# Linear attention into a three-matrix FFN on one core: w3 @ w_out moved from tile 0 to the front, and the start replanned

## The chip, the cores and the metric

The kernel runs on one core of a Trainium2 chip. The metric is the device time of one execution in microseconds (us). Engines are called PE (matmul), PEld (its weight load), DVE (VectorE), ACT (ScalarE), POOL (GpSimd) and SP (SyncE).

## The reference

Inputs are float32. q, k, v are [8 batches, 8 heads, 576 positions, 64]; w1, w2 are [512, 1024], w3 is [1024, 1024], w_out is [1024, 512].

```python
def phi(x, c, s):
    r = np.maximum(x, 0.0)
    return np.concatenate([r * c, r * s], axis=-1)      # 128 features
q_p, k_p = phi(q, cos_w, sin_w), phi(k, cos_w, sin_w)   # cos, sin of pi/2 * position / 576
kv  = np.einsum('bhsf,bhsd->bhfd', k_p, v)
z   = np.sum(k_p, axis=2)
num = np.einsum('bhsf,bhfd->bhsd', q_p, kv)
den = np.einsum('bhsf,bhf->bhs', q_p, z)[..., None] + 1e-06
x   = (num / den).transpose(0, 2, 1, 3).reshape(4608, 512)
out = (((x @ w1) * (x @ w2)) @ w3) @ w_out              # [4608, 512]
```

## The kernel before

**The algebra.** w3 @ w_out is computed once ("w34", 1024 x 512), so that a token costs three products: x @ w1, x @ w2 and their elementwise product @ w34. All matmuls are bfloat16 with float32 sums in PSUM.

**Attention.** A batch's 576 positions are five chunks, four of 128 and one of 64. Per chunk, `features` makes cos * relu on DVE and sin * relu on ACT (`kp`, `qp`), `prep_v` copies v beside a column of ones (`va`), and `kv_chunk` adds eight heads' 65-column products into PSUM. After the fifth chunk the sums are cast to `kvs`, one half on ACT, one on DVE. `q_tr` transposes a chunk of `qp` on PE (or a DMA does, `transpose_q`), the copy out of PSUM is `qpT`; `num` multiplies it with `kvs` and normalises on DVE (`den`, its reciprocal, `xblk`); `x_tr` transposes `xblk` on PE, copied to `xT` by ACT or DVE, or by a DMA on SP's queue for batches 2 and later. With `in_two`, `num` uses two FFN banks and normalises each by itself.

**FFN.** Nine tiles of 512 tokens. `ffn_groups(t)` is a generator: it issues a group of matmuls and yields. For each of eight column blocks `jc` there is x @ w1 (cast by ACT to `asb`) and x @ w2 (multiplied with `asb` by DVE into `abT`), and then four output blocks against `w34b`, each in two groups of four matmuls. Tile 0 and tile 1 take their first products in halves of 256 tokens (`on_half`), tile 0 some of them in quarters of 128, so that they can start on the first chunks of x. FFN results use four PSUM banks in turn (`ffn_tile`).

**w34 in the kernel before.** Inside tile 0, after its products, `w34_mm(jp, part)` runs eight blocks of eight 512-column matmuls. `w3_tr(jp)` transposes w3's row block jp by eight PE transposes into `pst`, and DVE copies them to `w3T`. ACT casts each sum to `w34b`.

**Order.** The schedule is manual: every engine works in the order in which the program issues its instructions. `slots[g]` is a list of calls made after FFN group g; `at(s, ...)` and `plan(b, ...)` put the attention steps of later batches into slots. Tile 0 has 40 groups and every later tile 24. `plan` takes slot lists: kf and qf for the features of k and q, vc for `prep_v`, kv for `kv_chunk`, nu for `num`, xt for `x_tr`.

**Loads.** POOL issues the loads, which cast float32 to bfloat16 on the way; only batch 0's k (`kf`, float32) comes on SP's queue. The order is k, v, q of batch 0, then the first halves of w1 and w2, then (after the first chunk's `xblk`) the rest of w1 and w2, w3 in row blocks with w_out between, batch 1. `plan_loads` places later batches' loads in slots, held back until ACT reaches that point (`hold_back`).

**The start.** 27 matmuls on zeros (`idle_mms`, into the tile `unread`) run on PE while the first loads come; then kv of batch 0 (`kv_first`), q's transposes, `num` and `x_tr` of chunk 0, and tile 0.

Of the kernel before, what the change touches and what calls it, by code (L numbers as in the profile page):

```python
# [10 lines left out]
FP32 = mybir.dt.float32  # L11
# [5 lines left out]
P = 128  # L17
H, S, D = 8, 576, 64
F = 2 * D
NCH = 5  # L20
# [48 lines left out]
def kernel(  # L69
# [30 lines left out]
    first = [ctx.enter_context(ExitStack()) for _ in range(2)]  # L100
    ps_idle = first[1].enter_context(tc.tile_pool(name="ps_idle", bufs=1, space=bass.MemoryType.PSUM))
    ps_first = first[0].enter_context(tc.tile_pool(name="ps_first", bufs=1, space=bass.MemoryType.PSUM))
# [42 lines left out]
    def load_wout(half):  # L145
        nc.gpsimd.dma_start(out=woutb[:, ts(half, 4), :],
                            in_=moe_w_out[ts(half, 512), :].rearrange("(c p) m -> p c m", p=P))

    k0 = raw[0, "k"] = wst.tile([P, H, NCH, D], FP32, name="kf")
    q0 = raw[0, "q"] = ld.tile([P, H, NCH, D], BF16, name="qs", bufs=2)  # L150
    v0 = raw[0, "v"] = ld.tile([P, H, NCH, D], BF16, name="vs")
    load_first(nc.sync, k0, k)
    load_first4(nc.sync, k0, k)
    load_first(nc.gpsimd, v0, v)
# [19 lines left out]
    unread = ps_idle.tile([P, 512], FP32, name="unread")  # L174
    kva = ps_idle.tile([P, 512], FP32, name="kva")

    def idle_mms(n):

        for _ in range(n):
            nc.tensor.matmul(unread[:, :], lhsT=zeros[:, 0:128], rhs=zeros[:], start=True, stop=True)  # L180

    idle_mms(27)
    cosv, sinv = _trig_tables(nc, const)
    identb = const.tile([P, P], BF16, name="identb")
    load_first4(nc.gpsimd, v0, v)
    load_first(nc.gpsimd, q0, q, 0, 2)
    make_identity(nc, identb[:])
    load_first(nc.gpsimd, q0, q, 2, 2)
    def load_w12(c0, n):
        nc.gpsimd.dma_start(out=w1b[:, :, ds(c0, n)], in_=w1v[:, :, ds(c0, n)])  # L190
        nc.gpsimd.dma_start(out=w2b[:, :, ds(c0, n)], in_=w2v[:, :, ds(c0, n)])
# [4 lines left out]
    nc.gpsimd.dma_start(out=w1b[:, :, ds(512, 256)], in_=w1v[:, :, ds(512, 256)])  # L196

    def other_loads(behind):

        seen = sm.tile([P, 1], BF16, name="seen", bufs=1)  # L200
        nc.gpsimd.tensor_copy(out=seen[:], in_=behind)
        nc.gpsimd.dma_start(out=w2b[:, :, ds(512, 256)], in_=w2v[:, :, ds(512, 256)])
        load_w12(768, 256)
        for jp in range(2):
            load_w3(jp, 1)
            load_wout(jp)
        for jp in range(2, 4):
            load_w3(jp, 1)
        load_w3(4, 2)
        load(1, "k")  # L210
        load_w3(6, 2)

# [11 lines left out]
    w34_acc = {}  # L224

# [11 lines left out]
    def order_of(b):  # L237

        return [0, 1, 2, 3, 4] if b % 2 == 0 else [4, 0, 1, 2, 3]
# [48 lines left out]
    def prep_v(b, c):  # L288
        R = ROWS[c]
        eng = nc.vector if b < 2 else nc.gpsimd  # L290
        eng.tensor_copy(out=feat_of(b)[2][:R, c, :, 0:D], in_=raw[b, "v"][:R, :, c, :])  # L291
# [15 lines left out]

    def kv_first():

        kp, qp, va = feat[0]  # L310
        kvs = sm.tile([P, H, D + 1], BF16, name="kvs", bufs=2)
        kvb = ps_att.tile([P, 2, 512], FP32, name="pnum")
        halves = (kva[:, :], kvb[:, 0, :])
        for c in range(NCH):
            for h in range(H):
                nc.tensor.matmul(halves[h // 4][:, ds((h % 4) * 65, 65)], lhsT=kp[:, c, h, :],
                                 rhs=va[:, c, h, 0:D + 1], start=(c == 0 and h % 4 == 0),
                                 stop=(c == NCH - 1 and h % 4 == 3))
        att_of(0)["kvs"] = kvs
        yield  # L320
        for half in range(2):
            nc.scalar.copy(out=kvs[:, 4 * half:4 * half + 4, :], in_=halves[half][:, 0:260])
        yield
# [23 lines left out]
    def num(b, c, chain=True, in_two=False):  # L347
# [4 lines left out]
        if b == 0 and c == 0:  # L352
            nt = ps_first.tile([P, 2, 512], FP32, name="pfirst")
        else:
            pool = more_att[0] if more_att and order_of(b).index(c) % 2 == 0 else ps_att
            nt = None if in_two else pool.tile([P, 2, 512], FP32, name="pnum")
# [86 lines left out]
    ffn_tiles = [0]  # L443

    def ffn_tile():
        pool = ps_ffn[ffn_tiles[0] // 2 % 2]
        ffn_tiles[0] += 1
        return pool.tile([P, 512], FP32, name="ffnps")

    def ffn_groups(t):  # L450
# [14 lines left out]

        def on_half(half):

            if half == 1 and t == 0:
                banks = [(ffn_tile(), ffn_tile()) for _ in range(2)]
                for quarter in range(2):  # L470
                    for pair, (a, b) in enumerate(banks):
                        for i in range(2):
                            for ps, w in ((a, w1b), (b, w2b)):
                                products(ps[:, ds(256 * i + 128 * quarter, 128)], w, 2 * pair + i,
                                         ds(256 + 128 * quarter, 128))
                        if quarter == 1:
                            multiply(a, b, pair, half)
                        if quarter == 0 or pair == 1:
                            yield
                return  # L480
            for pair in range(2):
                a, b = ffn_tile(), ffn_tile()
                if pair == 0 and t == 0:
                    for quarter in range(2):
                        for i in range(2):
                            for ps, w in ((a, w1b), (b, w2b)):
                                products(ps[:, ds(256 * i + 128 * quarter, 128)], w, i,
                                         ds(256 * half + 128 * quarter, 128))
                            if half == 0 and quarter == 0 and i == 0:
                                yield  # L490
                        if quarter == 0:
                            yield
                else:
                    for ps, w in ((a, w1b), (b, w2b)):
                        for i in range(2):
                            products(ps[:, ts(i, 256)], w, 2 * pair + i, ts(half, 256))
                        if w is w1b and (t == 1 or half == 0):
                            yield
                multiply(a, b, pair, half)
                yield  # L500

        if t < 2:
            yield from on_half(0)
            yield from on_half(1)
        for jc in range(4 if t < 2 else 0, 8):
# [9 lines left out]
        if t == 0:  # L515
            for jp in range(8):
                for part in range(2):
                    w34_mm(jp, part)
                    yield
            early.close()  # L520
            holds.append(ctx.enter_context(tc.tile_pool(name="hold", bufs=HELD,
                                                        reuse_waits="tile")))
# [28 lines left out]
    slots = [[] for _ in range(40 + 24 * (NT - 1))]  # L551
# [31 lines left out]
    for c in range(NCH):  # L583
        prep_k(0, c)
    for c in range(NCH):
        prep_v(0, c)
    kv_steps = kv_first()
    next(kv_steps)
    q0f = feat[0][1]
    features(0, q0f, q0, 0, scalar_heads=4)  # L590
    next(kv_steps)
    prep_q(0, 1)
    idle_mms(2)
    q_tr_halves(0, 0)
    prep_q(0, 2)
    idle_mms(1)
    num(0, 0)
    q_tr(0, 1, evac=False)[1]()
    other_loads(att[0]["x"][0][:, 0, 0, 0:1])
    features(0, q0f, q0, 3, sin=False)  # L600
    features(0, q0f, q0, 3, cos=False)
    idle_mms(2)
    x_tr(0, 0, by_vector=True)
    num(0, 1)
    q_tr(0, 2, evac=False)[1]()
    ps_ffn = []
    for stack in first:
        stack.close()
    for i in range(2):
        ps_ffn.append(ctx.enter_context(tc.tile_pool(name=f"ps_ffn{len(ps_ffn)}", bufs=2,  # L610
                                                     space=bass.MemoryType.PSUM)))


    at(1, lambda: x_tr(0, 1, by_vector=True), lambda: q_tr(0, 3, evac=False)[1](), lambda: num(0, 2))
    at(3, lambda: x_tr(0, 2), lambda: num(0, 3))
    at(5, lambda: x_tr(0, 3))
    at(6, lambda: features(0, q0f, q0, 4))
    at(23, lambda: transpose_q(0, 4))
    at(7, lambda: load(1, "qv"), lambda: load(2, "q"))
    at(29, lambda: num(0, 4))  # L620
    at(11, lambda: feature_buffers(1))
    at(29, lambda: x_tr(0, 4))

    for jp, s in enumerate((13, 16, 18, 20, 22, 24, 26, 28)):
        at(s, lambda jp=jp: w3_tr(jp))

    plan(1, kf=(24, 25, 26, 27, 28), vc=(31, 31, 32, 32, 32), kv=(33, 33, 33, 34, 34),
         qf=(29, 30, 30, 31, 31), nu=(35, 36, 38, 39, 42), xt=(37, 38, 40, 42, 42))
    for c, s in zip(order_of(1), (31, 32, 34)):
        at(s, lambda c=c: q_tr(1, c))  # L630
    at(43, no_more_by_pe)
# [59 lines left out]
```

## Time and profile before

| what | value |
|---|---|
| median of 3 runs | 249.66 us (249.4 to 249.91) |
| profiled execution, its own time | 249.83 us |
| its span, first to last instruction | 248.1 us |
| granted TensorE clock, mean | 0.999 |
| DVE, ACT, POOL busy | 137.5, 130.5, 93.3 us |
| x @ w1 and x @ w2, PE (L456) | 2 x 75.5 us |
| output products, PE (L526) | 65.1 us |
| w3 @ w_out, PE (L231) and w3's transposes (L219) | 15.8 and 4.9 us |
| matmuls on zeros, PE (L180) | 32, 9.4 us |
| HBM read, written | 38.80 MB, 9.44 MB |

A group row tells line, engine, operation, tiles, shape and count, then busy time, mean ns of one, idle time before it and what ended that. A row of the order in time tells start and length in us first; rows of the chain too. A row of the waits tells who waited for whom, us in total, how often, and the longest. A matmul's length holds the pipeline's tail, so the pace of queued matmuls is read from start to start: a 512-column one 0.216 us, a 128-column transpose 0.056, a 65-column one 0.032.

### The profile page before, as it was taken

The page shows a single profiled execution, that of the slowest core. Times are in us where ns is not written, and L with a number is a line of the kernel's source. Part 1 is how long each engine was busy: PE and PEld are TensorE (multiplying, and loading weights), DVE is VectorE, ACT ScalarE, POOL GpSimd, SP SyncE. Part 2 cuts the span into 40 slices and gives each one's busy share as a digit, 9 for nine tenths or more (in the row PEclk, how much of TensorE's full clock was granted, in tenths as well). Part 3 has the DMA queues.
Part 4 walks back from the last instruction along what each step waited for, and adds up shares of the span by engine and source line. Part 5 has one row for each costly group of instructions (what it writes and reads, how often), then busy time and mean ns, then how long its engine had stood idle before and what let it go on. Part 6 is the DMA issues. An engine that isn't in the chain of part 4 may idle for free.

```text
span 248.1 us, 5041 instructions
## 1 busy us (share of the span) xinstructions
PE 240.9 (97%) x1872; PEld 130.1 (52%) x1872; DVE 137.5 (55%) x336; ACT 130.5 (53%) x266; POOL 93.3 (38%) x196
## 2 busy tenths in 40 slices
PE   8899999999999999999999999999999999999993
PEld 3479445566964445545554545455445544444442
DVE  7875653668967544656665475657455644403320
ACT  2675323867933963476447654754575234334322
POOL 7655342124412351217122612352222006968600
PEclk9999999999999999999999999999999999999999
DMA  6999999999989979999999999999996427999925
GB/s 199 178 194 199 201 194 204 198 194 175 144 151 148 167 117 151 130 142 103 170 160 173 117 160 169 160 119 144 157 138 112 91 42 242 264 290 276 295 55 127
DMA packets 84744, 41.22 MB, mean 166 GB/s; under 512 B 52336, under 2 KB 81264, under 8 KB 84720
## 3 DMA queue, kind: packets, MB, share of 16 engines
q0 software_dynamic: 35472, 27.20, 71.6%
q1 hardware_dynamic: 49088, 13.57, 36.9%
q8 instruction: 14, 0.23, 0.4%
q10 hardware_dynamic: 160, 0.13, 0.2%
q14 instruction: 10, 0.08, 0.1%
HBM read 38.80 MB, written 9.44 MB: 194 GB/s over the span
## 4 chain that ended last, share of the span: by engine, by line
PE 88%; DMA 6%; DVE 1%; issue 1%; POOL 1%; ACT 0%; ACTq 0%; POOLq 0%
PE ffnps L456 48%; PE ffnps L526 24%; PE ffnps L231 6%; PE pnum L299 4%; PE pnum L359 4%; DMA qs<-in_q_dram 3%; DMA ks<-in_k_dram 3%; PE pst L219 1%; PE pst L330 1%; PE pst L411 1%; POOL vs L127 0%; PE ffnps L542 0%; ACT osb L544 0%; DVE xblk L377 0%; DVE abT L513 0%
## 5 line engine op out<-in xcount | busy, mean ns | idle before, releaser
L456 PE MATMUL ffnps<-xT,w1b 128*128 128x512 bf16 (+2 forms) x344 | 75.5, 344 | 0.2 <-issue 0.2
L456 PE MATMUL ffnps<-xT,w2b 128*128 128x512 bf16 (+2 forms) x344 | 75.5, 344 | 0.0
L513 DVE TENSOR_TENSOR abT<-asb,ffnps 128x512 bf16<-128x512 bf16 x64 | 43.9, 686 | 53.5 <-PE ffnps L456 51.6
L526 PE MATMUL ffnps<-w34b,abT 128*128 128x512 bf16 x280 | 65.1, 379 | 0.1
L509 ACT CAST asb<-ffnps 128x512 bf16<-128x512 f32 x64 | 37.4, 585 | 50.2 <-PE ffnps L456 45.4
L456 PEld LDWEIGHTS <-w2b 128*128 128x128 bf16 x344 | 30.9, 98 | 27.3
L456 PEld LDWEIGHTS <-w1b 128*128 128x128 bf16 x344 | 30.7, 98 | 26.3 <-issue 0.6
L561 POOL COPY seen<-mark 1x1 bf16<-1x1 bf16 x50 | 9.0, 180 | 85.7 <-ACT mark L559 85.7
L526 PEld LDWEIGHTS <-abT 128*128 128x128 bf16 x280 | 26.0, 98 | 28.3 <-DVE abT L513 0.6
L533 ACT COPY osb<-ffnps 128x512 f32<-128x512 f32 x35 | 20.5, 585 | 34.7 <-PE ffnps L526 34.7
L268 ACT ACTIVATE qp<-qs,sinv 128x512 bf16<-128x512 bf16 (+2 forms) x40 | 28.1, 715 | 1.9 <-DMA qs<-in_q_dram 1.9
L377 DVE TENSOR_TENSOR xblk<-pnum,den 128x512 bf16<-128x512 f32 (+1 forms) x37 | 25.6, 691 | 1.3
L291 POOL COPY va<-vs 128x512 bf16<-128x512 bf16 (+1 forms) x30 | 17.8, 627 | 22.0 <-DMA vs<-in_v_dram 20.0
L268 ACT ACTIVATE kp<-ks,sinv 128x512 bf16<-128x512 bf16 (+1 forms) x35 | 25.0, 718 | 1.5 <-DMA ks<-in_k_dram 1.3
L441 POOL DMA_DIRECT2D out_dram<-osb x42 | 22.2, 533 | 2.4 <-issue 2.3
L359 PEld LDWEIGHTS <-qpT 128*128 128x128 bf16 x320 | 15.4, 98 | 8.7 <-DVE qpT L344 0.6
L375 DVE TENSOR_SCALAR den<-pnum 128x8 f32<-128x8 f32 (+1 forms) x37 | 6.1, 164 | 22.5 <-PE pnum L359 22.4
L264 DVE TENSOR_SCALAR qp<-qs,cosv 128x512 bf16<-128x512 bf16 (+1 forms) x40 | 16.1, 411 | 0.6 <-DMA qs<-in_q_dram 0.6
L231 PE MATMUL ffnps<-woutb,w3T 128*128 128x512 bf16 x64 | 15.8, 380 | 0.0
L359 PE MATMUL pnum<-kvs,qpT 128*128 128x65 bf16 x296 | 15.8, 194 | 0.0
L299 PEld LDWEIGHTS <-kp 128*128 128x128 bf16 x280 | 11.4, 98 | 4.1
L264 DVE TENSOR_SCALAR kp<-ks,cosv 128x512 bf16<-128x512 bf16 (+1 forms) x35 | 12.9, 379 | 0.1
(86 smaller groups left out, 181.3 us busy)
## 6 DMA issues: line engine op xcount, KB each, us to landing
out_dram<-osb POOLq DMA_DIRECT2D x16, 256.0 KB, 4.4
out_dram<-osb POOLq DMA_DIRECT2D x24, 128.0 KB, 4.0
qs<-in_q_dram POOLq DMA_DIRECT2D x9, 256.0 KB, 7.8
ks<-in_k_dram POOLq DMA_DIRECT2D x7, 320.0 KB, 6.2
qs<-in_q_dram POOLq DMA_DIRECT2D x7, 320.0 KB, 6.0
vs<-in_v_dram POOLq DMA_DIRECT2D x7, 320.0 KB, 5.5
ks<-in_k_dram POOLq DMA_DIRECT2D x7, 256.0 KB, 7.5
vs<-in_v_dram POOLq DMA_DIRECT2D x7, 256.0 KB, 5.3
```

The costliest lines, as they stand in the source:

```text
L231: nc.tensor.matmul(acc[:, :], lhsT=w3T[:, lc, :], rhs=woutb[:, lc, :], start=(lc == 0), stop=(lc == 7))
L264: nc.vector.tensor_scalar(out=dst[:R, c, :, 0:D], in0=src[:R, :, c, :], scalar1=0.0, scalar2=cosv[:R, at:at + 1], op0=ALU.max, op1=ALU.mult)
L268: nc.scalar.activation(out=dst[:R, c, 0:n, D:F], in_=src[:R, 0:n, c, :], func=ACTF.Relu, scale=sinv[:R, at:at + 1], bias=0.0)
L299: nc.tensor.matmul(kvt[:, h // 4, ds((h % 4) * 65, 65)], lhsT=kp[:, c, h, :], rhs=va[:, c, h, 0:D + 1], start=(i == 0 and h % 4 == 0), sto ...
L359: nc.tensor.matmul(banks[h // 4][:, ds((h % 4) * 65, 65)], lhsT=qpT[:, h, ds(at, 128)], rhs=kvs[:, h, :], start=True, stop=True)
L377: nc.vector.tensor_tensor(out=xblk[rows, g], in0=n4[:, :, :, 0:D], in1=den[rows, g].unsqueeze(3).to_broadcast([R, G, 4, D]), op=ALU.mult)
L441: on.dma_start(out=rows[:, :, cols], in_=osb[64 * i:64 * i + rows.shape[0], :, cols])
L456: nc.tensor.matmul(out, lhsT=w[:, kc, ts(jc, 128)], rhs=x[:, kc, tok], start=(kc == 0), stop=(kc == 3))
L509: nc.scalar.copy(out=asb[:], in_=aT[:, :])
L513: nc.vector.tensor_mul(out=abT[:, jc, :], in0=asb[:], in1=bT[:, :])
L526: nc.tensor.matmul(ops[:, :], lhsT=abT[:, jc, ts(ms, 128)], rhs=w34b[:, jc, :], start=(jc == 0), stop=(jc == 7))
L533: nc.scalar.copy(out=osb[:, ms % 2, :], in_=ops[:, :])
```

## The change

w3 @ w_out is computed ahead of batch 0's attention. w_out's first 256 rows come as float32 on SP's queue (`wof`) and are cast by ACT. w3's first two row blocks come in four pieces of 256 columns, taken by `w34_first` as they land: four transposes, a copy (ACT for two pieces, DVE for two), four matmuls, with matmuls on zeros between. Blocks 2 to 7 follow as whole rows. k of batch 0 is loaded by POOL with a cast, behind block 6. Its features are made within the w34 loop behind block 5, `prep_v` (chunks 3 and 4 on ACT) and `kv_chunk` in block 7. Then come q's transposes, `num` of chunks 0 and 1, `x_tr` of chunk 0, and tile 0. Tile 0 takes quarters of 128 tokens for column blocks 0 and 1 only, and whole tiles for blocks 2 to 7; it has 25 groups. Batches 1 to 3 get other slots; from batch 4 on slots are those of before less 15. Matmuls on zeros: 10 at the start and 13 in `w34_first`.

```diff
+    def w34_first():
+        acc = [ffn_tile() for _ in range(2)]
+        for i in range(4):
+            pst = ps_tr.tile([P, 8, 128], BF16, name="pst")
+            for n in range(4):
+                nc.tensor.transpose(pst[:, n, :], w3b[:, n % 2, ds(256 * i + 128 * (n // 2), 128)], identb[:])
+            w3T = wst.tile([P, 8, 128], BF16, name="w3T", bufs=2)
+            if i == 0:
+                nc.scalar.copy(out=woutb[:, 0, :], in_=wof[:, 0, :])
+            copy = nc.scalar.copy if i < 2 else nc.vector.tensor_copy
+            copy(out=w3T[:, 0:4, :], in_=pst[:, 0:4, :])
+            if i == 0:
+                nc.scalar.copy(out=woutb[:, 1, :], in_=wof[:, 1, :])
+            idle_mms(2 if i else 1)
+            for n in range(4):
+                lc = 2 * i + n // 2
+                nc.tensor.matmul(acc[n % 2][:, :], lhsT=w3T[:, n, :], rhs=woutb[:, lc, :],
+                                 start=(lc == 0), stop=(lc == 7))
+            idle_mms(2 if i < 3 else 0)
+        for jp in range(2):
+            nc.scalar.copy(out=w34b[:, jp, :], in_=acc[jp][:, :])
...
-    load_first(nc.sync, k0, k)
-    load_first4(nc.sync, k0, k)
-    load_first(nc.gpsimd, v0, v)
+    nc.sync.dma_start(out=wof[:], in_=wout_rows(0))
+    for i in range(2):
+        load_w3_columns(i)
...
-    idle_mms(27)
+    idle_mms(10)
+    make_identity(nc, identb[:])
+    load_wout(1)
     cosv, sinv = _trig_tables(nc, const)
+    load_w3_columns(2)
+    load_wout(2)
+    load_w3_columns(3)
+    load_wout(3)
+    for jp in range(2, 7):
+        load_w3(jp, 1)
+    load_first(nc.gpsimd, k0, k)
+    load_first4(nc.gpsimd, k0, k)
+    load_w3(7, 1)
+    load_first(nc.gpsimd, v0, v)
     load_first4(nc.gpsimd, v0, v)
...
+    w34_first()
+    w3_tr(2)
+    feat_of(0)
+    for jp in range(2, 8):
+        w34_mm(jp, 0)
+        if jp < 7:
+            w3_tr(jp + 1)
+        if jp == 5:
+            w34_mm(jp, 1)
+            for c in range(NCH):
+                prep_k(0, c)
+        elif jp == 7:
+            for c in range(NCH):
+                prep_v(0, c)
+            for c in range(NCH):
+                kv_chunk(0, c, c)
+            w34_mm(jp, 1)
+        else:
+            w34_mm(jp, 1)
     features(0, q0f, q0, 0, scalar_heads=4)
     prep_q(0, 1)
     q_tr_halves(0, 0)
+    q_tr(0, 1, evac=False)[1]()
+    num(0, 0)
     prep_q(0, 2)
+    q_tr(0, 2)
+    num(0, 1, in_two=True)
+    x_tr(0, 0)
+    prep_q(0, 3)
+    at(0, lambda: x_tr(0, 1), lambda: q_tr(0, 3, evac=False)[1](), lambda: num(0, 2))
+    at(2, lambda: x_tr(0, 2), lambda: num(0, 3))
+    at(3, lambda: x_tr(0, 3, by_vector=True))
+    at(4, lambda: features(0, q0f, q0, 4), lambda: transpose_q(0, 4))
+    at(3, lambda: load(1, "kqv"), lambda: load(2, "q"))
+    at(14, lambda: num(0, 4))
...
-    plan(1, kf=(24, 25, 26, 27, 28), vc=(31, 31, 32, 32, 32), kv=(33, 33, 33, 34, 34),
-         qf=(29, 30, 30, 31, 31), nu=(35, 36, 38, 39, 42), xt=(37, 38, 40, 42, 42))
-    for c, s in zip(order_of(1), (31, 32, 34)):
+    plan(1, kf=(13, 14, 15, 16, 17), vc=(20, 20, 20, 20, 20), kv=(21, 21, 21, 21, 21),
+         qf=(17, 18, 18, 19, 19), nu=(22, 23, 24, 26, 29), xt=(24, 24, 26, 28, 29))
+    for c, s in zip(order_of(1), (19, 20, 22)):
         at(s, lambda c=c: q_tr(1, c))
-    plan(2, kf=(36, 37, 38, 40, 41), vc=(41, 42, 43, 44, 45), kv=(46, 46, 46, 47, 47),
-         qf=(40, 41, 42, 43, 44), nu=(48, 50, 52, 54, 57))
+    plan(2, kf=(27, 28, 29, 30, 31), vc=(30, 31, 32, 33, 34), kv=(34, 34, 34, 35, 35),
+         qf=(27, 28, 29, 30, 31), nu=(35, 37, 39, 41, 44))
...
+        def first_columns(half):
+            a, b = ffn_tile(), ffn_tile()
+            for quarter in range(2):
+                for i in range(2):
+                    for ps, w in ((a, w1b), (b, w2b)):
+                        products(ps[:, ds(256 * i + 128 * quarter, 128)], w, i,
+                                 ds(256 * half + 128 * quarter, 128))
+                    if half == 0 and quarter == 0 and i == 0:
+                        yield
+                if quarter == 0:
+                    yield
+            multiply(a, b, 0, half)
+            yield
...
-        for jc in range(4 if t < 2 else 0, 8):
+        for jc in range((2, 4)[t] if t < 2 else 0, 8):
```

## The prediction

> **What bounds the kernel now.** I read the page's engine shares first, then the waits of PE, then the start in order of time, then the long stretch by windows. TensorE is the engine that sets the end, and only the start has holes.
>
> ```profile
> PE 240.9 (97%) x1872; PEld 130.1 (52%) x1872; DVE 137.5 (55%) x336; ACT 130.5 (53%) x266; POOL 93.3 (38%) x196
> ```
>
> ```profile
> PE unread L180 <- DVE zeros L156: 1.2, 1, 1.2
> PE kva L316 <- DVE va L291: 1.0, 1, 1.0
> PE pst L411 <- DVE xblk L377: 0.3, 1, 0.3
> ```
>
> These are the whole span's large waits of PE: 2.5 us, all before 15 us. But busy isn't useful. The windows restricted to the `unread` matmuls show 9.43 us of them before 15.9 us, when the first real FFN matmul starts. Useful until then: 40 kv matmuls at 0.032 us from start to start (1.3), 24 q transposes at 0.056 (1.35), 16 num at 0.032 (0.5), one x transpose group (0.22): 3.4 us. So **12.5 of the first 15.9 us are lost**, and from there PE runs without a hole of note to 243.1. The same sum over the changed kernel gives the forecast: useful work hardly changes, so I count lost PE time only.
>
> **Prices.** PE, ACT and DVE each work in the order written out by hand, so a row's place in the queue matters as much as its time. The joint between attention and FFN in the trace of before gives the hand-overs, and a block of w3 gives its price:
>
> ```profile
> 12.54 0.76 DVE L344 COPY qpT<-pst 128x512 bf16<-128x512 bf16 x2 [0.18 <-PE pst L343]
> 13.70 0.17 DVE L375 TENSOR_SCALAR den<-pfirst 128x8 f32<-128x8 f32 x1
> 14.13 0.69 DVE L377 TENSOR_TENSOR xblk<-pfirst,den 128x512 bf16<-128x512 f32 x1
> 14.14 1.01 ACT L333 COPY qpT<-pst 128x1024 bf16<-128x1024 bf16 x1 [0.32 <-PE pst L330]
> 14.88 0.40 PE L411 MATMUL pst<-identb,xblk 128*128 128x128 bf16 x4 [0.34 <-DVE xblk L377]
> 48.71 1.94 ACT L268 ACTIVATE qp<-qs,sinv 64x512 bf16<-64x512 bf16 x3
> ```
>
> ```profile
> 33.26 0.45 PE pst L219 x8
> 33.71 1.82 PE ffnps L231 x8
> 35.53 0.45 PE pst L219 x8
> ```
>
> One reads: a normalisation takes 1.13 us (13.70 to 14.83), a sine 0.61 when queued (three in 1.94, with 0.1 of tail), a hand-over 0.05, a PE group's result comes 0.16 after its last issue, a w3 block takes 2.27. ACT casts of 512 columns take 0.58 (0.48 queued), DVE's w3T copy 0.69.
>
> **Loads.** Cast loads land one behind another. Taking each transfer's issue and landing from the trace and counting float32 MB read, all between w1b's first (3.93 MB, 14.27) and w3b's last (15.2 MB, 44.21) lie near 3.8 us + MB / 0.376 per us; q's first half (2.88 MB) lands at 11.52, the line says 11.5. In the new order: first w3 columns 5.9, block 2 at 13.6, then 1.4 a block, k 22.3, v 26.8, q 28.2 and 29.6, first weight pair 32.4, last 41.1, batch 1's k, q, v 44.2, 47.4, 50.5. Each is ahead of its use below (by 1 us for w3 blocks, 2.8 for k, 0.6 for v, 3 for q, 5 or more from the weights on), so nothing is charged for them after the first columns; late loads would cost us for us past those margins. POOL, which all these issues pass, spends 0.55 to 1.05 on each of some 28 and has eight in flight, as before; SP has only w_out's first rows ahead of its transposes. [...]
>
> **A, four column steps.** Ten idle matmuls: nine fill 1.20 to 5.0 (0.43 each), the tenth ends at 5.2. Columns at 5.9. A step is transposes 0.22, tail and hand-over 0.21, copy 0.58 on ACT (0.42 on DVE), hand-over 0.05, four matmuls 0.86, idle matmuls 0.45 behind it (those ahead lie beside the copy): 2.4, 2.4, 2.2 and, without the last idle pair, 1.8. End 14.7. Useful in it: 16 transposes and 16 matmuls, 4.35. **Lost 10.4.** Bounds: 9.7 if the columns are there at 5.2, 11.8 if they come at 7.3 (kf's time in the trace). I take the line, whose nearest check is kf itself, 6.39 for twice the bytes.
>
> **B, blocks 2 to 7.** Block 2 has no cover: 0.16 + 0.05 + 0.69 + 0.05 = **0.95 lost**. Then 2.27 each, as before: w34's work moves at equal price. w34_mm(7, 0) ends at 28.4.
>
> **C, kv of batch 0.** ACT gets the five k sines behind w34b 5, whose matmuls end at 25.1, though k landed at 22.3. Queue: 25.3 + 0.48 + 5 x 0.61 + 0.48 (w34b 6) + 0.48 (va 3) + 0.58 (va 4) = 30.4. PE reaches chunk 3 at 29.2: it waits 0.8, chunk 4 0.2, chunk 0 0.2. **Lost 1.2**; bounds 0 and 1.6. k's cosines get cheaper on DVE (375 against 749 ns, bf16 for float32), beside this path.
>
> **D, the joint.** w34 ends at 31.6. q's first sine stands behind w34b 7: 0.21 + 0.48 + 0.51 + 0.05 = 1.25 of hole. Two half transposes, 0.5 more for their bank, q_tr(0, 1), num(0, 0). Then q_tr(0, 2) needs a sine that ACT does behind the 1.01 copy and a cosine that DVE does behind the whole normalisation of chunk 0: 1.7. After num(0, 1) and x_tr, the x copy has no cover: 0.16 + 0.05 + 0.58 + 0.05 = 0.84. FFN starts at 37.9; 6.3 us with 2.1 useful, **4.2 lost**. Before, q's cosine 2 stood ahead of the normalisation, and the whole joint lost 2.5 (10.03 to 15.92 with 3.4 useful): that is the lower bound, 5 the upper.
>
> **E, tile 0's first columns.** With only two column blocks to multiply between x pieces (0.44 to 0.89 us of PE), each x piece is awaited: chunk 1's two-part normalisation (1.56 us, behind the qpT copy) 0.7, chunk 2's copy behind a product's cast 0.8, chunk 3 0.4 and 0.7. **Lost 2.6**; bounds 1 and 4. Before, the same places held twice the matmuls and lost nothing.
>
> **F, num(0, 4).** Its DMA transpose goes out at about 47.5, when loads fill the queue; PE asks at 54.4. Landings in the trace under such load took 9.5, 7.4 and 6.1 us: loss 0 to 2.7, I take 7.5 us, so **0.7**.
>
> **G, into tile 1.** num(1, 0) and its x_tr now have one output group between them, where before there were two:
>
> ```profile
> 57.27 0.42 PE L359 MATMUL ffnps<-kvs,qpT 128*128 128x65 bf16 x8
> 57.53 1.03 PE L526 MATMUL ffnps<-w34b,abT 128*128 128x512 bf16 x4
> 58.39 0.39 PE L411 MATMUL pst<-identb,xblk 128*128 128x128 bf16 x4
> 58.62 1.03 PE L526 MATMUL ffnps<-w34b,abT 128*128 128x512 bf16 x4
> 59.48 0.39 PE L411 MATMUL pst<-identb,xblk 128*128 128x128 bf16 x4
> ```
>
> The block came from DVE 2.0 us after num's start, PE would be back after 1.3: 0.7. Then tile 1 begins behind a transposition instead of two groups later: 0.6. Chunk 2's x_tr likewise comes 0.5 us before its block is there, and its copy has no group behind it: 0.8 more. **Lost 2.7**, bounds 1 and 3.5.
>
> **H, batch 2.** num(2, 0) sits in kv's last slot, with the kvs casts bare: 0.16 + 0.05 + 0.44 + 0.05 = **0.7**, bounds 0 and 1.5. From tile 2 on the slots are those of before less 15: nothing.
>
> **Sum.** 10.4 + 0.95 + 1.2 + 4.2 + 2.6 + 0.7 + 2.7 + 0.7 = 23.5 lost, against 12.5: +11.0. On the profiled execution's 249.83 us that is 260.8; the median of the runs is 0.17 lower, so **260.7 us**.
>
> **Clock.** The first nine idle matmuls started 0.43 us apart, the next 0.225, and after the 0.96 hole at 9.07 matmuls ran at full pace; the windows grant 1.00 throughout. My longest hole is 1.7, nearly twice that, so the trace can't exclude a drop. [...]
>
> **Rivals.**
> *Joints close up* (0.14): C to H lose only what before's joint lost, 2.5. Lost 13.9, +1.4: 251 us; half-way cases reach 255. For it: each is a wait under 1.7 us. Against: each follows from a queue order that the diff writes out.
> *The start is filled after all* (0.05, the faster case): the column steps run at PE's pace, since the idle matmuls ahead of each copy cover it. Then A loses 5.2 + 13 x 0.225 = 8.1, B nothing, the joint 2.5, the rest nothing: 10.6, -1.9, 247.8 us. From my A and B on, the sign turns only if C to H lose under 1.2 us in sum (12.5 - 10.4 - 0.95); D alone is three times that.
> *The clock falls in A* (0.08): 29 matmuls at 0.43 for 0.216 add 6.2: 267 us.
> *My forecast* (0.73): all low ends together take 8.3 off, all high ends add 7.6; not all will fall on one side, and two thirds of each give 255 to 266.
>
> 0.2%, or 0.5 us, is about what a measurement of this kernel can tell from no change. Faster 0.05, same 0.02 (the joints' best end), slower 0.93. The range runs from 253.5, into the rival of closed joints, to 265.5.
>
> **What would show it.** Right: FFN's first matmul near 38 us; w34's blocks at 2.27 from 16 us on; PE's waits named kv on ACT's va, pst on ACT qp and DVE qp, ffnps on xT; spare matmuls cut to 23. Wrong: FFN starting before 35, or w34 waiting on DMA w3b in the middle (then loads rule, not queues), or starts of 0.43 us among w34's matmuls.

## The result and the profile after

The changed kernel takes 261.61 us (259.80 to 262.46, 4 runs) against 249.64 before: a ratio of 1.047, 95% interval 1.041 to 1.053, 12.0 us slower. The forecast was 260.7 with 253.5 to 265.5. The profiled execution takes 260.84 us, 11.0 more than the profiled one of before.

The page's shares after: PE is busy as long as before (241.1 and 240.9 us) and the span is 11 us longer.

```profile
PE 241.1 (93%) x1802; PEld 129.3 (50%) x1831; DVE 135.7 (52%) x338; ACT 132.4 (51%) x271; POOL 97.5 (38%) x202
```

PE's waits (who waits for whom, us in total, times, longest): where before had three rows above 0.25 us, there are now a dozen, and the releasers are ACT and DVE. Only one of them is a wait for a load, that of the first columns.

```profile
PE ffnps L463 <- ACT xT L427: 2.2, 4, 0.7
PE pst L347 <- DVE qp L297: 1.8, 1, 1.8
PE pst L360 <- ACT qp L301: 1.1, 1, 1.1
PE pst L425 <- DVE xblk L391: 1.0, 3, 0.5
PE ffnps L264 <- DVE w3T L230: 0.8, 1, 0.8
PE pnum L333 <- ACT va L325: 0.7, 1, 0.7
PE pst L241 <- DMA w3b<-in_moe_w_dram: 0.6, 1, 0.6
PE pnum L373 <- ACT kvs L338: 0.5, 1, 0.5
```

The joint in order of time (start, length, engine, line), PE first, then ACT and DVE, which explain its two large holes:

```profile
33.42 0.62 PE L360 MATMUL pst<-identb,qp 128*128 128x128 bf16 x8 [1.08 <-ACT qp L301]
...
37.01 0.93 PE L347 MATMUL pst<-identb,qp 128*128 128x128 bf16 x8 [1.82 <-DVE qp L297]
37.73 0.65 PE L373 MATMUL ffnps<-kvs,qpT 128*128 128x65 bf16 x8
...
39.48 0.59 PE L463 MATMUL ffnps<-xT,w1b 128*128 128x128 bf16 x4 [0.67 <-ACT xT L427]
```

```profile
32.37 0.58 ACT L267 CAST w34b<-ffnps 128x512 bf16<-128x512 f32 x1 [0.49 <-PE ffnps L264]
32.85 1.12 ACT L301 ACTIVATE qp<-qs,sinv 128x256 bf16<-128x256 bf16 x2
34.97 1.01 ACT L350 COPY qpT<-pst 128x1024 bf16<-128x1024 bf16 x1 [1.00 <-PE pst L347]
35.88 0.72 ACT L301 ACTIVATE qp<-qs,sinv 128x512 bf16<-128x512 bf16 x1
```

```profile
35.67 0.69 DVE L391 TENSOR_TENSOR xblk<-pnum,den 128x512 bf16<-128x512 f32 x1
36.28 0.59 DVE L297 TENSOR_SCALAR qp<-qs,cosv 128x512 bf16<-128x512 bf16 x1
```

q's first sine starts at 32.85, behind w34's last cast, though q landed at 29.0; chunk 2's cosine starts at 36.28, behind chunk 0's normalisation, though that data landed at 30.5. The transposes at 37.01 wait for it. They also take 0.72 us from first to next work instead of 0.45: the clock has fallen. The windows show the granted clock (third number from the end; the second of a row is its length, then PE, PEld, DVE, ACT and POOL busy) over three stretches of 3.41 us:

```profile
33.72:37.13 3.41, 1.30 (x25) 1.12 (x23) 2.32 (x6) 1.88 (x3) 2.36 (x4) 1.00 1.57 191
37.13:40.54 3.41, 2.74 (x31) 2.57 (x30) 2.29 (x8) 1.20 (x2) 1.67 (x3) 0.50 1.44 196
40.54:43.95 3.41, 2.99 (x59) 2.85 (x58) 1.73 (x5) 2.59 (x4) 0.00 (x0) 1.00 1.40 200
```

Tile 1's start after, beside the rows of before: one output group between num and its x transposition, then FFN straight behind.

```profile
66.62 0.42 PE L373 MATMUL ffnps<-kvs,qpT 128*128 128x65 bf16 x8
66.88 1.02 PE L515 MATMUL ffnps<-w34b,abT 128*128 128x512 bf16 x4
...
68.78 0.29 PE L425 MATMUL pst<-identb,xblk 128*128 128x128 bf16 x2 [0.45 <-DVE xblk L391]
...
69.73 1.03 PE L463 MATMUL ffnps<-xT,w1b 128*128 128x256 bf16 x8 [0.41 <-ACT xT L427]
```

### The profile page after: what moved, and what is told of

The parts are those of the page before. It is cut to its first block, busy times and chain, and to the rows that moved or that the text cites. A ratio compares the mean times of both kernels' runs of the same rounds, so it can differ in the third digit from the quotient of the medians.

```text
span 259.1 us, 4941 instructions
## 1 busy us (share of the span) xinstructions
PE 241.1 (93%) x1802; PEld 129.3 (50%) x1831; DVE 135.7 (52%) x338; ACT 132.4 (51%) x271; POOL 97.5 (38%) x202
## 4 chain that ended last, share of the span: by engine, by line
PE 85%; DVE 5%; ACT 4%; DMA 2%; issue 2%; ACTq 0%; DVEq 0%; POOLq 0%
PE ffnps L463 47%; PE ffnps L515 22%; PE pnum L373 4%; PE pnum L333 3%; PE ffnps L264 3%; DMA w3b<-in_moe_w_dram 2%; PE ffnps L253 2%; DVE xblk L391 1%; ACT kp L301 1%; PE pst L347 1%; PE pst L228 1%; ACT xT L427 1%; PE pst L425 1%; DVE den L390 1%; DVE abT L469 1%
## 5 line engine op out<-in xcount | busy, mean ns | idle before, releaser
L463 PE MATMUL ffnps<-xT,w1b 128*128 128x512 bf16 (+2 forms) x316 | 73.9, 353 | 3.4 <-ACT xT L427 2.2
L510 DVE TENSOR_TENSOR abT<-asb,ffnps 128x512 bf16<-128x512 bf16 x66 | 45.1, 685 | 52.7 <-PE ffnps L463 49.4
L506 ACT CAST asb<-ffnps 128x512 bf16<-128x512 f32 x66 | 38.5, 583 | 50.9 <-PE ffnps L463 44.8
L515 PE MATMUL ffnps<-w34b,abT 128*128 128x512 bf16 x272 | 63.7, 379 | 0.3
L463 PEld LDWEIGHTS <-w1b 128*128 128x128 bf16 x328 | 29.9, 98 | 30.3 <-issue 4.0
L301 ACT ACTIVATE kp<-ks,sinv 128x512 bf16<-128x512 bf16 (+1 forms) x40 | 28.1, 716 | 1.6 <-DMA ks<-in_k_dram 1.6
L301 ACT ACTIVATE qp<-qs,sinv 128x512 bf16<-128x512 bf16 (+2 forms) x40 | 28.2, 713 | 0.0
L297 DVE TENSOR_SCALAR qp<-qs,cosv 128x512 bf16<-128x512 bf16 (+1 forms) x40 | 16.7, 423 | 0.0
L333 PEld LDWEIGHTS <-kp 128*128 128x128 bf16 x320 | 12.8, 98 | 5.5 <-issue 1.0
L297 DVE TENSOR_SCALAR kp<-ks,cosv 128x512 bf16<-128x512 bf16 (+1 forms) x40 | 14.5, 372 | 1.2 <-DMA ks<-in_k_dram 1.1
L333 PE MATMUL pnum<-va,kp 128*128 128x65 bf16 x320 | 13.6, 193 | 0.8 <-ACT va L325 0.7
```

The source lines that it names most:

```text
L297: nc.vector.tensor_scalar(out=dst[:R, c, :, 0:D], in0=src[:R, :, c, :], scalar1=0.0, scalar2=cosv[:R, at:at + 1], op0=ALU.max, op1=ALU.mult)
L301: nc.scalar.activation(out=dst[:R, c, 0:n, D:F], in_=src[:R, 0:n, c, :], func=ACTF.Relu, scale=sinv[:R, at:at + 1], bias=0.0)
L333: nc.tensor.matmul(kvt[:, h // 4, ds((h % 4) * 65, 65)], lhsT=kp[:, c, h, :], rhs=va[:, c, h, 0:D + 1], start=(i == 0 and h % 4 == 0), sto ...
L463: nc.tensor.matmul(out, lhsT=w[:, kc, ts(jc, 128)], rhs=x[:, kc, tok], start=(kc == 0), stop=(kc == 3))
L506: nc.scalar.copy(out=asb[:], in_=aT[:, :])
L510: nc.vector.tensor_mul(out=abT[:, jc, :], in0=asb[:], in1=bT[:, :])
```

## The experiments

The theory: PE loses time because steps that feed it stand late in the hand-written queues of ACT and DVE, or have no PE work behind them. There are two rivals: that loads set the pace, and that the granted clock does. Differences below are against the changed kernel's 261.6, where a run of it is one of four with 2.7 us between them, so under a microsecond they are read with the profiles. The kernel before, run beside them, had medians of 249.8 to 250.3, and 249.6 beside the changed kernel: by up to 0.7 us a difference can be that of the batch of runs.

### Joint: q's features earlier

```diff
+            features(0, q0f, q0, 0, scalar_heads=4); prep_q(0, 1); prep_q(0, 2)
             w34_mm(7, 1)
...
-    features(0, q0f, q0, 0, scalar_heads=4); prep_q(0, 1)
     q_tr_halves(0, 0)
     q_tr(0, 1, evac=False)[1]()
     num(0, 0)
-    prep_q(0, 2)
```

> The changed kernel with q's features of chunks 0 to 2 issued ahead of the last half of w34's block 7, so that ACT and DVE find them ahead of the w34 cast, of the 1.0 us copy and of chunk 0's normalisation. Queue order (my theory): the two holes of 1.25 and 1.98 us in the joint close, FFN starts near 36.0 instead of 39.5 us, and the time is 258.2 (257.5 to 259) against 261.6. Loads rule (rival): q and the first weights, landed at 29.0, 30.5 and 33.1 us, are what the joint waits for; FFN starts at 39 or later and the time stays at 261 or above. Clock (second rival): the joint stays thin enough for a stretch at half clock; FFN then starts earlier by 2.5 only and the time is about 259.5.

Measured: 259.5 us (257.9 to 260.6), 2.1 less, which is the clock rival's number. The profile tells more. The hole of 1.8 is gone and the first has become 0.4:

```profile
PE pst L360 <- DVE qp L297: 0.4, 1, 0.4
PE ffnps L373 <- ACT qpT L350: 0.4, 1, 0.4
PE pst L241 <- DMA w3b<-in_moe_w_dram: 1.8, 1, 1.8
```

But in this execution, the slowest of the four, the first columns landed at 6.66 instead of 6.18, behind a hole of 1.8 us, and a stretch from 7.4 to 10.8 us ran at half clock. Counted from block 2's first product, FFN starts 20.2 us later instead of 22.8: 2.6 us came back. So the queues were the cause of the joint's holes, and the clock took part of the gain, though in stage A and not in the joint. Loads don't rule here: PE's only wait for one is the 1.8 us for the first columns.

### Batches 1 and 2 in the slots of before

`plan(1)`, `plan(2)`, q's transposes and `plan_loads` take the numbers of the kernel before, less 15 (and one feature of batch 3 comes a slot earlier):

```diff
-    plan(1, ... kv=(21, 21, 21, 21, 21), nu=(22, 23, 24, 26, 29), xt=(24, 24, 26, 28, 29))
+    plan(1, ... kv=(18, 18, 18, 19, 19), nu=(20, 21, 23, 24, 27), xt=(22, 23, 25, 27, 27))
-    plan(2, ... kv=(34, 34, 34, 35, 35), nu=(35, 37, 39, 41, 44))
+    plan(2, ... kv=(31, 31, 31, 32, 32), nu=(33, 35, 37, 39, 42))
```

> The changed kernel with batches 1 and 2 (and their loads) in the slots of the kernel before, less 15. Queue order: the holes at tile 1's start and before its second half (0.6 + 0.6 + 0.5 + 0.8) and the one ahead of batch 2's first num (0.9) close, and the time is 258.2 (257.5 to 259.2). Rival, loads rule: batch 1's k, q, v land at 44.7, 47.7 and 51.2 us, the earlier slots only move the waits to the features and kv of batch 1, and the time stays within 0.7 us of 261.6.

Measured: 257.8 us (257.1 to 258.6), 3.8 less, as the theory had it. From 60 to 95 us its PE shows no hole above 0.25 us; the waits for batch 1's loads that the rival expects don't appear (one new wait of 0.5 us, for a sine of q, does, ending at 58.1 us).

### The kernel before with the changed plans

The mirror of it: the kernel before, untouched but for the changed kernel's plans of batches 1 to 3, 15 slots later:

```diff
-    plan(1, ... kv=(33, 33, 33, 34, 34), nu=(35, 36, 38, 39, 42), xt=(37, 38, 40, 42, 42))
+    plan(1, ... kv=(36, 36, 36, 36, 36), nu=(37, 38, 39, 41, 44), xt=(39, 39, 41, 43, 44))
-    plan(2, ... kv=(46, 46, 46, 47, 47), nu=(48, 50, 52, 54, 57))
+    plan(2, ... kv=(49, 49, 49, 50, 50), nu=(50, 52, 54, 56, 59))
```

> The kernel before, with only the changed kernel's plans of batches 1 to 3 and their loads (15 slots later). Queue order: the holes at tile 1's start, in its halves and ahead of batch 2's first num appear here too, with nothing of w34 moved: 249.7 to 250.3 plus 3.4 = 253.4 (252.4 to 254.2). Rival: those holes come from what the moved start leaves behind on ACT and DVE; then the kernel before keeps its time within 0.7 us.

Measured: 253.7 us (253.5 to 253.8) beside 249.8, a ratio of 1.0154 (1.0131 to 1.0178): 3.9 us slower, with nothing of w34 moved. The waits of before's three rows are joined by the changed kernel's own:

```profile
PE pst L411 <- DVE xblk L377: 1.1, 3, 0.5
PE ffnps L456 <- ACT xT L413: 1.1, 2, 0.7
PE pnum L359 <- ACT kvs L304: 0.5, 1, 0.5
```

About a third of the loss thus belongs to the replanned slots alone.

### Matmuls on zeros in the joint

13 of them into an idle FFN bank (`spare`, two tiles of `ffn_tile()`):

```diff
+    spare_mms(4)
     q_tr_halves(0, 0)
...
     num(0, 0)
+    spare_mms(7)
...
     x_tr(0, 0)
+    spare_mms(2)
```

> The changed kernel with 13 matmuls on zeros put into the joint's holes (4, 7 and 2), into an idle FFN bank; no wait is changed. Clock theory: the stretch at half clock (37.1 to 40.5 us in the changed kernel's profile) goes, the FFN's first columns run at 0.055 us a matmul at once, and the time is 260.2 (259.5 to 260.8), with the runs within 0.8 us of each other and not 2.7. Queue order alone: the holes are the same, the time stays at 261.6 with the same spread.

Measured: 260.0 us (259.6 to 261.0). By the medians 1.6 us came back by adding work, and the spread went from 2.7 to 1.4 us, not quite to 0.8. In the profile no stretch at half clock is left; the same window as above:

```profile
33.72:37.13 3.41, 3.06 (x38) 2.01 (x37) 1.98 (x6) 1.65 (x3) 2.39 (x4) 1.00 1.57 191
37.13:40.54 3.41, 2.54 (x41) 1.83 (x38) 2.46 (x8) 1.79 (x3) 1.57 (x3) 1.00 1.44 197
```

The profiles give the clock a smaller price. The changed kernel copies tile 0's first output at

```profile
59.77 0.57 ACT L522 COPY osb<-ffnps 128x512 f32<-128x512 f32 x1
```

and this one, with FFN's first product and a new wait shown too, at

```profile
38.30 0.38 PE L463 MATMUL ffnps<-xT,w1b 128*128 128x128 bf16 x4 [0.24 <-ACT xT L427]
39.41 0.28 PE L425 MATMUL pst<-identb,xblk 128*128 128x128 bf16 x2 [0.39 <-DVE xblk L391]
59.05 0.57 ACT L522 COPY osb<-ffnps 128x512 f32<-128x512 f32 x1
```

From q's first transposes (33.42 and 33.18) FFN starts after 6.06 and 5.12 us, so 0.95 came back in the joint; but up to the first output it is 26.35 and 25.87, since the wait for chunk 1 of x, which half clock had hidden, now shows. So the clock is a real part of the loss beside the queues, of about 0.5 us in the profiled execution. Of the 1.1 us between the two profiled executions another 0.24 arose ahead of the joint and 0.4 past 100 us, where the edit changes nothing.

### Tile 0's first products as before

`first_columns` takes column blocks 0 to 3 as the kernel before did (its body is that of before's `on_half` for tile 0):

```diff
-        for jc in range((2, 4)[t] if t < 2 else 0, 8):
+        for jc in range(4 if t < 2 else 0, 8):
...
-    at(0, lambda: x_tr(0, 1), ...); at(2, lambda: x_tr(0, 2), ...); at(3, lambda: x_tr(0, 3, by_vector=True))
+    at(1, lambda: x_tr(0, 1, by_vector=True), ...); at(3, lambda: x_tr(0, 2), ...); at(5, lambda: x_tr(0, 3))
```

> The changed kernel with tile 0's first products as in the kernel before: column blocks 0 to 3 in halves and quarters, and the x transposes two slots apart. Queue order: the waits for chunks 2 and 3 of x (0.6 + 0.4 + 0.7) close, and the time is 260.0 (259.2 to 260.8). Rival: the chunks of x are late in themselves, because the joint's steps on ACT and DVE run behind; then the waits move to the next chunk and the time stays within 0.6 us of 261.6.

Measured: 259.7 us (258.8 to 261.2), 1.9 less. The waits for chunks 2 and 3 of x are gone and did not move on, even though this execution was at half clock from 36.2 to 43.0 us.

### k's features and v's copies

```diff
-        if jp == 5:
+        if jp == 4:
             w34_mm(jp, 1)
             for c in range(NCH): prep_k(0, c)
```

and v's chunks 3 and 4 copied by DVE.

> The changed kernel with k's features of batch 0 behind block 4 and not block 5, and v's chunks 3 and 4 copied by DVE. Queue order: kv's waits for ACT's va (0.9 + 0.3 us) close and all that follows comes 1.2 us earlier: 260.4 (259.6 to 261.2) against 261.6. Rival, loads rule: v lands at 27.1 and 27.6 us, 1.3 us ahead of kv, so nothing hides there; but if the ACT queue behind it (w34 cast, q's sines) sets the joint, the joint's hole grows by what kv saves and the time stays at 261.6.

Measured: 259.7 us (258.9 to 260.7), 2.0 less where 1.2 was expected. PE's waits for ACT's va are gone: from kv's first product to q's first transposes it takes 3.39 us instead of 4.55. The profiled execution doesn't explain the surplus, as it is the slowest of the four (260.67). Its columns landed 0.5 us sooner (5.64), but a piece of w_out that came later took that back (block 2 starts at 15.27 for 15.25). It kept full clock, and from q's first transposes to the first output takes 25.78 us for 26.35, as with the matmuls on zeros. Then it lost 1.1 us ahead of tile 5:

```profile
166.49 1.02 PE L462 MATMUL ffnps<-xT,w1b 128*128 128x512 bf16 x4 [1.12 <-ACT osb L521]
```

The copy that is named had ended at 166.0; a DMA transpose of x landed at 166.40.

### No matmuls on zeros behind the column steps

```diff
-            idle_mms(2 if i < 3 else 0)
```

> The changed kernel without the 7 matmuls on zeros behind the column steps (three pairs and the one of step 0 stays: six go). Queue order: three pairs of 0.43 us lie on the path, but the last w_out quarter lands at 13.0 and w3's block 2 at 14.3 us, so loads take over after 0.9 of the 1.3 us: 260.7 (260 to 261.5). Clock (rival): with fewer spare matmuls the stage falls to half clock for one or two stretches of 3.4 us and the time rises to 262.5 to 264.

Measured: 260.9 us (260.3 to 262.7), 0.75 less, near the theory by the median. In the profiled execution (260.97) nothing came back: from the first columns' transposes to block 2's it takes 9.29 us, and 9.02 in the changed kernel. What took the place of the spare work is a load:

```profile
PE ffnps L253 <- DMA woutb<-in_moe_w_out_dram: 1.1, 2, 0.7
PE pst L228 <- DMA w3b<-in_moe_w_dram: 0.2, 1, 0.2
```

Here the rival of the loads has its place: stage A can't be made shorter than w_out's last quarter and w3's block 2 allow (landed at 13.85 and 15.09 us here). The clock rival's fall in stage A didn't come. The joint's did, as in the changed kernel. It followed a stretch in which PE was busy for 1.55 of 3.41 us; the stretch before that, with 1.70, had kept full clock behind it:

```profile
29.90:33.31 3.41, 1.70 (x21) 0.87 (x20) 1.15 (x4) 2.42 (x6) 1.59 (x3) 1.00 1.46 196
33.31:36.72 3.41, 1.55 (x26) 1.37 (x27) 2.08 (x6) 2.19 (x3) 2.05 (x3) 1.00 1.57 191
36.72:40.13 3.41, 2.74 (x30) 2.57 (x31) 2.29 (x8) 1.21 (x2) 2.09 (x4) 0.50 1.45 196
```

### All four mends together

The edits of the joint, of the slots, of tile 0's first products and of k and v, in one kernel.

> The changed kernel with the joint's features ahead, batches 1 and 2 in the slots of the kernel before less 15, tile 0's first products as before, and kv's ACT waits removed, all together. Queue order: the lost times add, since they lie one behind another on PE: 261.6 less 3.3 (joint with its clock), 3.4 (plans), 1.6 (columns), 1.2 (kv) = 252.1 (251 to 253.2). The rest over the kernel before, some 2 us, is then stage A and block 2's bare copy. Rival, loads rule: as the start closes up, q (29.0 and 30.5 us) and the first weights (33.1) become what is awaited and no more than half of it comes back: 255 or more.

Measured: 253.0 us (252.2 to 253.2) beside 249.8, a ratio of 1.0118 (1.0084 to 1.0151). 8.6 of 12.0 us are back. The losses add (the four alone gave 9.8 in sum; here it is 8.6 beside a new wait of 1.4), and behind stage A loads don't stand in the way. A wait that the changed kernel had missed by a microsecond came up: PE now asks for batch 0's last q chunk before its DMA transpose has landed (issued 44.48, landed 51.82).

```profile
PE pnum L372 <- DMA qpT<-qp: 1.4, 1, 1.4
PE pst L241 <- DMA w3b<-in_moe_w_dram: 1.2, 1, 1.2
PE ffnps L264 <- DVE w3T L230: 0.8, 1, 0.8
```

### The holes filled with w34's last block

```diff
+    w34_mm(7, 0)
     q_tr_halves(0, 0)
     q_tr(0, 1, evac=False)[1]()
     num(0, 0)
+    w34_mm(7, 1)
     q_tr(0, 2)
-    num(0, 1, in_two=True)
     x_tr(0, 0)
+    num(0, 1, in_two=True)
...
-    at(14, lambda: num(0, 4))
+    at(15, lambda: num(0, 4))
```

on top of all four mends and of the column steps without their trailing spares.

> As the kernel with all four mends, and further: no matmuls on zeros behind the column steps, block 7's two halves put into the joint's holes (ahead of q's first transposes and ahead of chunk 2's), and num of batch 0's last chunk one slot later with its features two slots earlier (its DMA transpose was awaited for 1.4 us in the kernel with all four mends). Queue order: FFN starts near 34 us, 13 of these lost where the kernel before loses 12.5 of 15.9, and all else is gone: 250.2 (249.5 to 251), level with the kernel before. Loads rule, now in my theory too: the first weight pair lands at 33.1 to 33.4 us, so no order of queues brings FFN's start below that and the time cannot fall under 249. A rival says w34 first has a gain that the holes hid: then 248 or less.

Measured: 251.9 us (250.4 to 253.5, 9 runs), ratio 1.0064 (1.0034 to 1.0094). Better than all mends, but a miss of 0.9 us against the upper end given. In the profiled execution the columns landed at 7.06, the ten matmuls on zeros were over at 4.9, and half clock followed that hole:

```profile
3.96:7.37 3.41, 1.17 (x9) 0.46 (x7) 2.30 (x13) 0.62 (x1) 3.34 (x9) 1.00 1.08 127
7.37:10.78 3.41, 3.16 (x14) 1.18 (x11) 0.40 (x3) 1.34 (x3) 2.80 (x6) 0.50 1.11 161
```

### 16 matmuls on zeros at the start

The filled kernel, with:

```diff
-    idle_mms(10)
+    idle_mms(16)
```

> The filled kernel with 16 matmuls on zeros at the start instead of 10, so that PE is kept at work until the first w3 columns land (6.2 to 7.1 us in the profiles so far). Clock: in the filled kernel's profile the hole of 2.2 us ahead of the columns was followed by a stretch at half clock from 7.4 to 10.8 us; without that hole the stretch goes, the median falls by 0.4 to 1.0 us from 251.9 to 251.2 (250.7 to 251.6), and the spread of 3 us shrinks to 2 or less. Loads rule alone (rival): the columns' landing sets stage A whatever the clock, and the median stays at 251.9.

Measured: 251.2 us (249.9 to 252.5, 11 runs), ratio 1.0031 (1.0009 to 1.0052). The stretch at half clock is gone from the profile:

```profile
7.37:10.78 3.41, 3.11 (x20) 1.45 (x20) 0.40 (x3) 1.10 (x2) 2.80 (x6) 1.00 1.17 157
```

The median fell by 0.7 us, the number of the clock theory, but the two profiled executions take 251.82 and 251.76, and don't show that price. This one is 1.4 us ahead at tile 0's first output (54.02 for 55.41), 0.8 of it because the columns landed sooner (6.30 for 7.06), and then loses 1.1 to a DMA transpose of batch 2's q:

```profile
79.40 0.43 PE L371 MATMUL pnum<-kvs,qpT 128*128 128x65 bf16 x8 [1.12 <-DMA qpT<-qp]
```

The spread stayed at 2.5 us with granted clocks of 0.996 to 1.0, so part of it has another source. Such transposes are one: PE waited 1.4 us for one with all four mends, and ahead of tile 5, 0.09 us behind the landing of one of x each time, it lost 0.2 us in the changed kernel, 0.6 with q's features earlier and 1.1 with k's. Whether they make the whole spread stays open. This is the best version of the change: by the medians 1.2 us behind the kernel before (0.8 by the ratio), not ahead.

### The kernel before without its five matmuls on zeros in the joint

```diff
-    idle_mms(2)
     q_tr_halves(0, 0)
     prep_q(0, 2)
-    idle_mms(1)
     num(0, 0)
...
-    idle_mms(2)
     x_tr(0, 0, by_vector=True)
```

> The kernel before without the five matmuls on zeros that lie in its joint (2, 1 and 2); the 27 at the start stay. Clock: the joint's thin stretch then lets the granted clock fall for 3.4 us in part of the runs, FFN's first matmuls run at half pace, and the time rises by 0.5 to 1.5 us with a wider spread. Rival: those matmuls only filled holes and the clock doesn't depend on them; the time stays within 0.3 us.

Measured: 250.5 us (249.4 to 251.8) beside 250.0, ratio 1.0013 (0.9994 to 1.0032). Inconclusive: the median moved by the lower end of what was expected and the spread grew from 1.5 to 2.4 us, but the interval holds no change, and the profiled execution, the slowest of the twelve, kept full clock.

## Why the prediction was right

The signs came as named: kv waits for ACT's va, q's transposes for ACT and DVE, FFN for xT, and w34's blocks run at 2.27 us from 16.65 on. FFN's first product came at 39.48 for 38. Stage by stage, lost PE time in the profiled execution (start to start, less the useful 0.216, 0.056 and 0.032 us a matmul; records missing from the trace, 0.22 us each, not counted as lost):

| stage | predicted | measured | what the runs say |
|---|---|---|---|
| A, column steps | 10.4 | 10.9 | columns at 6.18 for 5.9; 5.6 to 7.1 in other runs |
| B, block 2's bare copy | 0.95 | 0.95 | unchanged in all variants |
| C, kv behind ACT | 1.2 | 1.2 | closed by earlier features and DVE copies |
| D, joint | 4.2 | 5.2 | holes as named, plus half clock |
| E, first columns | 2.6 | 2.1 | chunk 1's wait absent; 0.5 of it is half clock |
| F, num(0, 4) | 0.7 | 0 | transpose landed at 54.5, asked for at 55.5 |
| G, tile 1 | 2.7 | 2.5 | G and H: 3.8 less by the slots of before |
| H, batch 2 | 0.7 | 1.0 | kvs casts on ACT and DVE one behind another |
| sum | 23.5 | 23.9 | |

That the sum comes this close is partly luck: A and D were 1.5 us short together, E and F 1.2 us long.

**A and the loads.** The line 3.8 us + MB / 0.376 held to 0.9 us: block 2 landed at 14.3 for 13.6, k at 22.6 for 22.3, v at 27.6 for 26.8, q at 29.0 and 30.5 for 28.2 and 29.6, the weights at 33.1 to 41.6. PE awaited no load but the first. The column pieces and w_out quarters landed 0.7 to 1.7 us apart, each 4.7 to 6.3 us after its issue, so each one's time from issue to landing overlapped those of the pieces beside it.

**D and E: the clock.** This is the step that was mis-sized. I gave the joint no price for the clock and kept a fall of it as a rival placed in A, at 6.2 us. That a hole of 1.7 us costs no clock was not shown: the longest in the trace of before, behind its first matmuls, is 0.96. The clock fell in the joint, for 3.41 us, and that costs about 1 us there: 6.06 us from q's first transposes to FFN, where the two runs that kept full clock with the joint's order unchanged (k's features, matmuls on zeros) take 5.11 and 5.12. In its place E's wait for chunk 1 (0.7) didn't show, since PE itself came late; so 0.5 to 0.6 us are left up to tile 0's first output (1.6 by the medians of the matmuls on zeros). A fall in A came in the run with q's features earlier, and stretched the way from the first columns to block 2 from 9.02 to 10.36 us: 1.3, not 6.2. In the 3.41 us before the fall in the changed kernel's joint PE was busy for 1.30, and its longest hole was 1.82: the clock fell there without a longer one.

**F.** The landing under load was the right uncertainty (0 to 2.7); the draw was the low end in the changed kernel and 1.4 in the one with all mends.

**The rival of closed joints** (251 us) is what the mends reach: 253.0, and 251.2 with the last two steps. It was refuted for the change as written only by the order of its queues, which was the ground given. **The faster rival** was 247.8; the best version found is at 251.2. FFN's first weights land at 33.1 us with 20.8 us of work to do until then, so about 12.3 us must be lost, against 12.5 before. That the two orders are level at best for this reason is argued from landings, not shown; the best version starts FFN at 34.8 us, 2.0 behind the landing of its own first weights (32.8), so there the loads don't set that start.

## What to carry to other kernels

When PE is the engine that sets the end, write the change down as PE time lost and walk every new hand-over through the hand-written queues of the feeding engines (q's first sine started 3.8 us after its data had landed, behind w34's last cast); here that gave the total to 1 us and most stages to 0.5. Moving work to the front of a load-bound start bought nothing by itself here, as the loads behind it moved back by about its bytes (6.3 MB, 16.7 us at 0.376 MB per us; FFN's first weight pair landed at 33.1 us for 15.6); what decided was whether the steps between arrival and first product had other matmuls beside them. A slot table's distances are part of the change: one group fewer between a result and its use cost 3.9 us in all.

## What the runs showed of the hardware that I had not expected

- The granted clock fell to half in six of the ten profiles of the changed kernel and its variants, each time for 3.41 us, and for two such stretches on end in the run with tile 0's first products. With each of these traces cut into stretches of 3.41 us at the fall, PE was busy for 1.17 to 1.55 us in the stretch ahead of it, with no hole longer than 2.3 us. The thinnest stretch that full clock followed had 1.70. In the run with k's features earlier the joint was as thin (1.29 us from 34.00 to 37.41) and the clock did not fall; what sets the two cases apart was not shown.
- The first load through POOL's queue in the changed kernel and its variants (0.13 MB written) landed 4.4 to 5.8 us after its issue, from execution to execution. The loads behind it didn't simply move along: the execution with the first columns at 5.64 had block 2 at 15.22, the one with 7.06 had it at 14.67.
- A DMA transpose landed 2.3 to 9.5 us after its issue in the profile of the kernel before and 2.3 to 9.0 in that of the changed one, and PE lost 0.2 to 1.4 us at once where a run came to need one early.
- By the medians, adding 13 useless matmuls to a kernel that PE bounds made it 1.6 us faster; between the profiled executions it is 1.1, of which 0.5 is traced to the clock.
